# An inverse transform with cosine and sine parts held apart for half of the tokens, and mirrored tokens read backwards

## The chip, the cores and the metric

The kernel runs on one core of one Trainium2 chip. A core has a matrix engine (PE; its weight loads are listed as PEld), a vector engine (DVE), a scalar engine (ACT), a general engine (POOL) and an engine that issues transfers (SP). They run side by side, each takes its own instructions in order, and they wait for each other on semaphores. PE writes its results to PSUM, eight banks per partition, from where DVE or ACT copy or combine them; POOL and the transfers reach only SBUF. The metric is the device time of one execution in microseconds (us).

## What is computed

Attention with eight heads, and then a mixing layer that convolves along the sequence by Fourier transforms. The layer is where the change lies.

```python
def _moe_ref(x, w_proj, filter_fft, w_out):        # x: batch 4, 768 tokens, 512 channels
    proj = x @ w_proj
    x1, x2, x3 = proj[..., :D], proj[..., D:2*D], proj[..., 2*D:]
    X2 = np.fft.rfft(x2, n=S, axis=1)
    H = np.fft.rfft(filter_fft, n=S, axis=0)[None, :, :]
    x2_conv = np.fft.irfft(X2 * H, n=S, axis=1)
    y = x1 * x2_conv * x3
    return y @ w_out
```

The attention before it: scores of 768 by 768 per head, causal, and for five of the heads cut to 4 first tokens and a window of 64; exponentials, division by the row sum, product with v. All inputs are float32 in memory; the kernel computes with bfloat16 operands.

## The kernel before

**Tiling.** There are 16 head pairs (four per batch), `n` = 0 to 15, and after four of them one batch `b` of the mixing layer. For a pair, q and k are loaded, cast and transposed (T, E), scores go to PSUM in chunks (sc), ACT takes exponentials (ex), DVE masks them (mk), PE multiplies with v (at), DVE divides (rec, nm). Differences and sums of the two halves of the tokens (fd, fe and, for later pairs, fA, fS, fb, fr) go through the forward transform (W), and the same attention output is transposed for the projections (tn, te).

**The mixing layer of a batch.** The spectrum X (L1125, three pairs of tiles) is copied out (Xe) and multiplied with the filter's spectrum (pa, pb, pc), which gives P. Then, for each of four blocks `cb` of 128 channels:
- x1 and x3, projections of 768 tokens (L1160), two groups of four matmuls each;
- c, the inverse transform (L1190): two groups `r` of three matmuls, whose moving operand is the table Gi, 384 tokens wide. Group 0 gives the part of the even frequencies, group 1 that of the odd ones, each for the first 384 tokens;
- ce (a copy of group 0 from PSUM, L535 or L541) and cv (L1201): the sum of both parts is the convolution at the first 384 tokens, their difference at the last 384. They go to `conv`, for which the program lends the opening's buffer, so the trace names it turns (and the copy angle);
- g (L1179: x1 by x3) and y (L544: conv by that product) give gy; in block 3 y multiplies conv by x1 first and g (L1183) then by x3; the output matmuls (o, L1225, L1220) take gy of all four blocks, oe copies, st stores.

**What sets the order.** All operations are written as small functions with names (`c3.2.1` is batch 3, block 2, group 1), and one long table, FAST, gives the sequence in which they are issued. A letter behind a name sets the engine where there is a choice (v DVE, s ACT, p POOL, d transfer), a number behind @ which of four PSUM buffers of two banks is used from there on. Each engine gets its instructions in the order of the table. No scheduler changes it.

**The opening.** Until the first X, the tables of cosines and sines are made: DVE computes angles, wrapped angles (wrap, L676) and their size (L681), ACT takes sines (L689) and then, with another function table loaded, exponentials. The inverse table Gi comes from PE transposes of the forward one (Gt, L729) and copies (Ge). SP loads q, k and v; POOL issues the load of the filter (lfilt, L739) and of the projection weights (lw, L747). Seven blank matmuls (L580) stand at three places among the first operations. A small check of the head kinds (chk, L629 to L637, and gd at the end) decides if a general version has to run afterwards.

## Time and profile before

| | |
|---|---|
| time, median of 3 runs | 185.87 us (185.37 to 186.39) |
| profiled execution, its span | 186.0 us |
| busy: PE, DVE, ACT, POOL | 171.6, 152.5, 142.2, 83.5 us |
| inverse matmuls (L1190) | 96, PE busy 18.7 us, mean 326 ns |
| cv (L1201) | 32, DVE busy 16.4 us, mean 547 ns |
| y on POOL (L544, f_gy from turns) | 7, 11.6 us, mean 1669 ns |
| mean granted PE clock | 0.993 |

A row of the groups gives line, engine, operation, what is written and read, shapes, count, then busy time in us and the mean of one in ns, and after a second bar the engine's idle time just before and what ended it. The mean of a matmul has its way through the array in it, during which the next one runs; how long one holds PE up is read from the chain of waits, where a row gives a start, the time that passes until the next and a count. Rows of a timeline have start, length and instruction.

### The profile page before, as it was taken

The numbers are of one execution on the slowest core, as the hardware profiler recorded it, in microseconds if no ns is written. First come the engines' busy times: TensorE is split into PE (matmuls) and PEld (weight loads), VectorE is DVE, ScalarE is ACT, GpSimd is POOL, SyncE is SP. The second block draws the span as 40 slices with busy tenths as digits, with TensorE's granted clock in tenths as the row PEclk, the third lists the DMA queues.
The fourth block names the chain that finished last, engine by engine and source line by source line (L and its number), as shares of the span: only waits on it lengthen the run. The fifth ranks groups of instructions, "written<-read, shape, count | busy, mean of one in ns | idle before, by whom it ended". The sixth has DMA issues, their size and how long they took to land.

```text
span 186.0 us, 4370 instructions
## 1 busy us (share of the span) xinstructions
PE 171.6 (92%) x1685; PEld 102.2 (55%) x1702; DVE 152.5 (82%) x297; ACT 142.2 (76%) x186; POOL 83.5 (45%) x99
## 2 busy tenths in 40 slices
...
GB/s 163 305 305 194 257 272 244 260 215 130 211 224 217 104 217 222 177 149 221 216 239 201 223 203 171 127 252 222 124 102 40 118 0 131 40 4 113 188 281 108
DMA packets 76836, 33.44 MB, mean 180 GB/s; under 512 B 66058, under 2 KB 73226, under 8 KB 76810
## 3 DMA queue, kind: packets, MB, share of 16 engines
...
q8 instruction: 14, 0.23, 0.6%
q10 hardware_dynamic: 146, 0.13, 0.2%
...
HBM read 24.64 MB, written 6.29 MB: 166 GB/s over the span
## 4 chain that ended last, share of the span: by engine, by line
PE 65%; DMA 16%; ACT 4%; DVE 4%; SPq 3%; POOL 3%; issue 2%; POOLq 0%
PE f_x_ps L1160 20%; PE f_out_ps L1225 10%; PE f_X_ps L1125 10%; DMA f_filt<-in_moe_filter_fft_dram 7%; PE f_c_ps L1190 7%; PE f_sc L961 6%; PE f_att L1021 4%; DMA f_qkT<-f_qk_bf 4%; DMA f_v_f<-in_v_dram 3%; SPq L898 3%; DMA qk_ahead<-in_q_dram 2%; PE f_xt_ps L1094 2%; PE f_F_ps L768 1%; POOL f_fo L544 1%; PE f_W_ps L1082 1%
## 5 line engine op out<-in xcount | busy, mean ns | idle before, releaser
L978 ACT ACTIVATE f_pT<-f_sc 128x1024 bf16<-128x1024 f32 (+2 forms) x68 | 58.3, 914 | 4.1 <-PE f_sc L972 2.1
L1160 PE MATMUL f_x_ps<-f_xT,f_wproj 128*128 128x384 bf16 x256 | 48.4, 326 | 0.1
L1160 PEld LDWEIGHTS <-f_wproj 128*128 128x128 bf16 x256 | 23.5, 98 | 15.6 <-issue 0.4
L961 PE MATMUL f_sc<-f_qkT 64*128 64x128 bf16 (+3 forms) x328 | 21.1, 242 | 2.2 <-ACT f_pT L978 0.8
L1125 PE MATMUL f_X_ps<-f_wproj,f_xh 128*128 128x512 bf16 x91 | 22.1, 379 | 0.3
L1225 PE MATMUL f_out_ps<-f_wout,f_gy 128*128 128x512 bf16 x85 | 22.0, 379 | 0.3
L544 POOL TENSOR_TENSOR f_gy<-turns,f_gy 128x768 bf16<-128x768 bf16 x7 | 11.6, 1669 | 20.8 <-DVE f_gy L1179 11.3
L1190 PE MATMUL f_c_ps<-f_Gi,f_P 128*128 128x384 bf16 x96 | 18.7, 326 | 0.1
L1021 PEld LDWEIGHTS <-f_pT 128*128 128x128 bf16 x472 | 16.4, 97 | 4.0 <-issue 1.5
L541 ACT COPY f_o<-f_out_ps 128x1024 f32<-128x1024 f32 (+2 forms) x15 | 11.5, 788 | 8.8 <-PE f_out_ps L1225 8.8
L961 PEld LDWEIGHTS <-f_qkT 64*128 64x128 bf16 x328 | 11.1, 94 | 12.6 <-issue 8.4
L1201 DVE TENSOR_TENSOR turns<-angle,f_c_ps 128x384 bf16<-128x384 f32 x32 | 16.4, 547 | 1.7 <-ACT angle L541 1.3
L1021 PE MATMUL f_att<-f_v_aug,f_pT 128*128 128x65 bf16 x392 | 17.3, 193 | 0.4 <-DVE f_attn L1038 0.4
L544 POOL TENSOR_TENSOR f_fo<-f_attn 128x384 bf16<-128x384 bf16 x11 | 10.9, 1003 | 14.6 <-PE f_W_ps L1082 12.2
L1038 DVE TENSOR_TENSOR f_attn<-f_att,f_recs 128x768 bf16<-128x768 f32 x16 | 15.3, 954 | 0.4
L541 ACT CAST f_X<-f_X_ps 128x1024 bf16<-128x1024 f32 x11 | 11.1, 1016 | 5.9 <-PE f_X_ps L1125 5.9
L544 POOL TENSOR_TENSOR f_br<-f_fo,f_uv 128x256 bf16<-128x256 bf16 x9 | 6.9, 766 | 18.7 <-DVE f_uv L544 9.1
L1125 PEld LDWEIGHTS <-f_xh 128*128 128x128 bf16 x96 | 8.9, 98 | 10.5 <-issue 1.0
L537 POOL CAST f_qk_bf<-qk_ahead 128x768 bf16<-128x768 f32 (+1 forms) x10 | 11.4, 1149 | 4.4 <-DMA qk_ahead<-in_k_dram 4.3
L1225 PEld LDWEIGHTS <-f_gy 128*128 128x128 bf16 x92 | 8.5, 98 | 8.8 <-issue 0.4
L541 ACT CAST f_xh<-f_W_ps 128x768 bf16<-128x768 f32 x12 | 9.5, 801 | 4.6 <-PE f_W_ps L1078 4.6
L1190 PEld LDWEIGHTS <-f_P 128*128 128x128 bf16 x96 | 9.1, 98 | 6.0
...
## 6 DMA issues: line engine op xcount, KB each, us to landing
...
qk_ahead<-in_k_dram SPq DMA_DIRECT2D x6, 384.0 KB, 6.4
qk_ahead<-in_q_dram SPq DMA_DIRECT2D x6, 384.0 KB, 6.2
...
```

Of the source, the lines that this page charges most:

```text
L537: nc.gpsimd.tensor_copy(out=out, in_=in_)
L541: nc.scalar.copy(out=out, in_=in_)
L544: (nc.gpsimd if now["engine"] == "p" else nc.vector).tensor_tensor(out, a, b, op)
L961: nc.tensor.matmul(sc[:, bank, col:col + 128 * cnt], lhsT=keys, rhs=qkT(n)[rows, 0, 128 * i:128 * (i + cnt)], start=(col == 0 or not biase ...
L978: nc.scalar.activation(out=pT(n)[:, c, :, 0:w], in_=held[f"sc.{n}.{c}"][:, :, 0:w], func=AF.Exp, scale=SCALE)
L1021: nc.tensor.matmul(att[:, hh, 65 * i:65 * i + 65], lhsT=pT(n)[:, c, bank, col:col + 128], rhs=values, start=(z == 0), stop=(z == len(here) ...
L1038: nc.vector.tensor_mul(attn(n).rearrange("p i hh d -> p hh i d"), rows[:, :, :, 0:64], recs()[:, n][:, :, :, None].to_broadcast([128, 2, N ...
L1125: nc.tensor.matmul(ps[:, u, :], lhsT=xh(b)[:, cc, chain, 128 * part:128 * part + 128], rhs=wproj()[:, cc, DM:2 * DM], start=(cc == 0), sto ...
L1160: nc.tensor.matmul(ps[:, s, 0:HS], lhsT=wproj()[:, cc, part * DM + cb * 128:part * DM + (cb + 1) * 128], rhs=xT(b)[:, cc, s * HS:s * HS + HS],
L1190: nc.tensor.matmul(ps[:, r, 0:HS], lhsT=P(b)[:, t, u, ch], rhs=Gi()[:, tile_no], start=(m == 0), stop=(m == 2))
L1201: fn(conv[:, half * HS:half * HS + HS], held[f"evs.{b}.{cb}"], held[f"c_ps.{b}.{cb}"][:, 1, 0:HS])
L1225: nc.tensor.matmul(ps[:, i % 2, :], lhsT=gy(b)[:, cb, i * 128:(i + 1) * 128], rhs=wout()[:, cb, :], start=(cb == 0), stop=(cb == NC - 1))
```

## The change

The inverse transform of 384 tokens is split once more. For token t and the mirrored token 384 - t, the cosine terms agree and the sine terms are opposite at even frequencies, and the other way round at odd ones, so it is enough to compute 194 tokens (MW = 384/2 + 2), with cosine and sine parts apart, side by side in one bank. A matmul group then has two matmuls of 194 columns (one into each part) and one of 388 (for the last, mixed tile of frequencies, into both). Then, per block:
- ce copies 2 x 194 columns, cv gives two times two parts, now in a new buffer `parts`;
- cd (new) adds the two parts: tokens 0 to 193 of each half;
- cm (new) subtracts them, reads them backwards (inner step -1) and writes tokens 194 to 383 of the other half (outer step -1);
- y and g are as they were.

Gi becomes [128, 2, 4 x 194]; its tiles for mixed frequencies hold zeros in half of the partitions (gz, ga). Twelve transposes make it instead of 18; Gt1 goes, and Ge is three copies instead of two.

```diff
--- before.py
+++ after.py
@@ -61,66 +61,68 @@
 FAST = """
...
-y3.3/v o2.3.1 o2.2.1 gd3@3 gd4 x33.3.0@0 x33.3.1 g3.3 o3.0.0@2 o3.1.0@3 o3.1.1 oe2.3/s oe3.1/s o3.0.1 o3.5.0@1 st2.3
...
+cv3.0.0 o2.1.0@2 o2.0.0 o2.0.1 cv3.1.0 x33.1.1@1 cd3.0/p cv3.1.1 o2.1.1 x33.1.0 c3.2.1@0 g3.2 cd3.1/v cm3.0/p oe2.1/s
...
 """
...
@@ -362,7 +364,8 @@
     pre["identity"] = pool.tile([128, 128], BF16, name="identity")
     pre["mtab"] = pool.tile([128, 6, 128], BF16, name="mtab")
     pre["turns"] = pool.tile([128, 3, HS], I32, name="turns")
-    pre["angle"] = pool.tile([128, 3, HS], FP32, name="angle")
+    pre["flat"] = pool.tile([128, 3 * HS + 8], FP32, name="angle")
+    pre["angle"] = pre["flat"][:, 0:3 * HS].rearrange("p (m t) -> p m t", m=3)
 
     blank, table, fcol, tcol, par, tfrac, quarter, identity, mtab, turns, angle = (
         (lambda name=name: pre[name]) for name in (
@@ -514,7 +517,10 @@
             return fn
         return put
 
-    shared = {"x1s0": pre["angle"][:, 2].bitcast(BF16).rearrange("p (s t) -> p s t", s=2), "evs0": pre["angle"][:, 0], "evs1": pre["angle"][:, 1],
+    MW = HS // 2 + 2
+    flat = pre["flat"]
+    shared = {"x1s0": flat[:, 4 * MW:4 * MW + HS].bitcast(BF16).rearrange("p (s t) -> p s t", s=2),
+              "evs0": flat[:, 0:2 * MW], "evs1": flat[:, 2 * MW:4 * MW],
               "conv0": pre["turns"][:, 0].bitcast(BF16), "conv1": pre["turns"][:, 1].bitcast(BF16)}
 
     def buf(name, shape, dtype, tag=None):
@@ -547,7 +553,7 @@
     blank = lambda: pre["blank"]
     table = lambda: pre["table"]
     G = C("G", [128, 6, NM, 128], BF16)
-    Gi = C("Gi", [128, 6, NM, 128], BF16)
+    Gi = C("Gi", [128, 2, 4 * MW], BF16)
     Gk = C("Gk", [128, 2, 2, 128], BF16)
     Gh = C("Gh", [128, NM, 128], BF16, "m20")
     par = lambda: pre["par"]
@@ -719,20 +725,47 @@
         nc.vector.tensor_scalar(out=Gh()[:, :, 0:65:64], in0=G()[:, 5, :, 0:65:64], scalar1=0.5, scalar2=None,
                                 op0=ALU.mult)
 
-    for part, tiles in enumerate(((0, 1, 2, 3), (4, 5))):
-        @op(f"Gt{part}")
-        def _(part=part, tiles=tiles):
-            ps = banks(f"Gi_ps{part}", BF16)
-            for z, t in enumerate(tiles):
-                for m in range(NM):
-                    col = (z % 2) * HS + 128 * m
-                    nc.tensor.transpose(ps[:, z // 2, col:col + 128], G()[:, t, m], identity())
-
-        @op(f"Ge{part}")
-        def _(part=part, tiles=tiles):
-            rows = len(tiles) // 2
-            ev(Gi()[:, tiles[0]:tiles[-1] + 1].rearrange("p (u t) m f -> p u (t m f)", u=rows),
-               held[f"Gi_ps{part}"][:, 0:rows, 0:2 * HS])
+    @op("Gt0")
+    def _():
+        ps = banks("Gi_ps", BF16)
+        for t in range(6):
+            for m in range(2):
+                col = (t % 3) * 256 + 128 * m
+                nc.tensor.transpose(ps[:, t // 3, col:col + 128], G()[:, t, m], identity())
+
+    def mirrored(lo, hi, part):
+        return held["Gi_ps"][lo:hi, :, 0:768].rearrange("p u (k c) -> p u k c", k=3)[:, :, part, 0:MW]
+
+    @op("Ge0")
+    def _():
+        ev(Gi()[:, :, 0:2 * MW].rearrange("p u (k c) -> p u k c", k=2), mirrored(0, 128, slice(0, 2)))
+
+    @op("Ge1")
+    def _():
+        ev(Gi()[0:64, :, 2 * MW:3 * MW], mirrored(0, 64, 2))
+
+    @op("Ge2")
+    def _():
+        ev(Gi()[64:128, :, 3 * MW:4 * MW], mirrored(64, 128, 2))
+
+    def zeros(at):
+        (nc.gpsimd if now["engine"] == "p" else nc.vector).memset(at, 0.0)
+
+    @op("gz0")
+    def _():
+        zeros(Gi()[0:64, :, 3 * MW:4 * MW])
+
+    @op("gz1")
+    def _():
+        zeros(Gi()[64:128, :, 2 * MW:3 * MW])
+
+    @op("ga0")
+    def _():
+        ev(Gi()[64:65, 1, 2 * MW:3 * MW], mirrored(64, 65, 2)[:, 1])
+
+    @op("ga1")
+    def _():
+        zeros(Gi()[64:65, 1, 3 * MW:4 * MW])
 
     @op("lfilt")
     def _():
@@ -1112,7 +1145,7 @@
         return buf(f"gy.{b}", [128, NC, S], BF16, f"gy{b % 2}")
 
     SPECTRUM = (((0, 0), (0, 1)), ((1, 0), (1, 1)), ((0, 2), (1, 2)))
-    INVERSE = (((1, 0, 3), (1, 1, 4), (2, 1, 5)), ((0, 0, 0), (0, 1, 1), (2, 0, 2)))
+    INVERSE = (((1, 0), (1, 1), (2, 1)), ((0, 0), (0, 1), (2, 0)))
 
     for b in range(B):
         for t in range(3):
@@ -1186,19 +1219,36 @@
                 @op(f"c{b}.{cb}.{r}")
                 def _(b=b, cb=cb, r=r, ch=ch):
                     ps = banks(f"c_ps.{b}.{cb}")
-                    for m, (t, u, tile_no) in enumerate(INVERSE[r]):
-                        nc.tensor.matmul(ps[:, r, 0:HS], lhsT=P(b)[:, t, u, ch], rhs=Gi()[:, tile_no],
-                                         start=(m == 0), stop=(m == 2))
+                    for m, (t, u) in enumerate(INVERSE[r]):
+                        to, at = ((0, MW), (MW, 2 * MW), (0, 2 * MW))[m], (0, MW, 2 * MW)[m]
+                        nc.tensor.matmul(ps[:, r, to[0]:to[1]], lhsT=P(b)[:, t, u, ch],
+                                         rhs=Gi()[:, 1 - r, at:at + to[1] - to[0]], start=(m == 0), stop=(m == 2),
+                                         skip_group_check=True)
 
             @op(f"ce{b}.{cb}")
             def _(b=b, cb=cb):
-                ev(buf(f"evs.{b}.{cb}", [128, HS], FP32, f"evs{cb % 2}"), held[f"c_ps.{b}.{cb}"][:, 0, 0:HS])
+                ev(buf(f"evs.{b}.{cb}", [128, 2 * MW], FP32, f"evs{cb % 2}"), held[f"c_ps.{b}.{cb}"][:, 0, 0:2 * MW])
 
             for half, fn in ((0, nc.vector.tensor_add), (1, nc.vector.tensor_sub)):
                 @op(f"cv{b}.{cb}.{half}")
                 def _(b=b, cb=cb, half=half, fn=fn):
-                    conv = buf(f"conv.{b}.{cb}", [128, S], BF16, f"conv{cb % 2}")
-                    fn(conv[:, half * HS:half * HS + HS], held[f"evs.{b}.{cb}"], held[f"c_ps.{b}.{cb}"][:, 1, 0:HS])
+                    parts = buf(f"parts.{b}.{cb}", [128, 2, 2, MW], BF16, f"parts{cb % 2}")
+                    fn(parts[:, half].rearrange("p w t -> p (w t)"), held[f"evs.{b}.{cb}"],
+                       held[f"c_ps.{b}.{cb}"][:, 1, 0:2 * MW])
+
+            @op(f"cd{b}.{cb}")
+            def _(b=b, cb=cb):
+                parts = held[f"parts.{b}.{cb}"]
+                conv = buf(f"conv.{b}.{cb}", [128, S], BF16, f"conv{cb % 2}")
+                two(conv.rearrange("p (s t) -> p s t", s=2)[:, :, 0:MW], parts[:, :, 0], parts[:, :, 1], ALU.add)
+
+            @op(f"cm{b}.{cb}")
+            def _(b=b, cb=cb):
+                parts = held[f"parts.{b}.{cb}"]
+                conv = buf(f"conv.{b}.{cb}", [128, S], BF16, f"conv{cb % 2}")
+                back = HS - MW
+                two(conv.rearrange("p (s t) -> p s t", s=2)[:, ::-1, MW:HS], parts[:, :, 0, back:0:-1],
+                    parts[:, :, 1, back:0:-1], ALU.subtract)
 
             @op(f"y{b}.{cb}")
             def _(b=b, cb=cb):
```

The FAST table is a new sequence of all operations, with other engine letters at many places. Counted over the table (before, then now): y 9 on DVE and 7 on POOL, then 13 and 3; ce 10 on ACT and 6 on DVE, then 13 and 3; the new cd 9 on DVE and 7 on POOL, cm 4 and 12. Before the first X there now stand also tn3, T6, sc4.5 and sc5.2, and no longer the three matmuls of blank1, which are issued behind the second block's inverse groups of batch 0.

The first place is the opening on DVE. Before, the wrapped angles and size stood together:

```order
L676 SCALAR_TENSOR_TENSOR angle_87<-turns_86,angle_87 128x384 x3
L681 TENSOR_SCALAR f_size_159<-angle_87 128x1152
L535 COPY f_qkT_0_166<-f_qkT_ps_0_137 128x768 x2
L624 TENSOR_SCALAR f_btab_187<-mtab_85 128x768
L535 CAST f_qk_bf_1_149<-qk_ahead1_69 128x768
```

Now (names with want, zeros, local, differs and differ are chk):

```order
L682 SCALAR_TENSOR_TENSOR angle_87<-turns_86,angle_87 128x384 x3
L635 MEMSET want_61 1x8
L638 MEMSET want_61 1x1 x3
L639 TENSOR_SCALAR zeros_59<-flags_58 1x16
L641 TENSOR_TENSOR local_60<-zeros_59 1x8
L642 TENSOR_TENSOR differs_62<-local_60,want_61 1x8
L643 TENSOR_REDUCE differ_63<-differs_62 1x1
L687 TENSOR_SCALAR f_size_164<-angle_87 128x1152
L541 COPY f_qkT_0_166<-f_qkT_ps_0_148 128x768
```

Eight small instructions of chk, one of which reads a loaded input (flags), came to stand ahead of size, and a memset of v_x between the two copies of qkT.

The second place is the last batch's blocks 2 and 3 on DVE, from the end of their inverse matmuls to the last product. Before (angle is the copy ce, turns is conv, f_x1s is x1):

```order
L535 COPY angle_87<-f_c_ps_3_2_2778 128x384
L1201 TENSOR_TENSOR turns_86<-angle_87,f_c_ps_3_2_2778 128x384 x2
L535 COPY angle_87<-f_c_ps_3_3_2807 128x384
L1201 TENSOR_TENSOR turns_86<-angle_87,f_c_ps_3_3_2807 128x384 x2
L544 TENSOR_TENSOR turns_86<-turns_86,f_x1s_3_3_2751 128x768
L661 TENSOR_SCALAR other_64<-f_rows_right_2842,differ_63 1x1
L1183 TENSOR_TENSOR f_gy_3_2641<-turns_86,f_x3_ps_3_3_2845 128x768
```

Now:

```order
L1236 TENSOR_TENSOR f_parts_3_2_2855<-angle_87,f_c_ps_3_2_2824 128x388 x2
L1236 TENSOR_TENSOR f_parts_3_3_2864<-angle_87,f_c_ps_3_3_2841 128x388 x2
L550 TENSOR_TENSOR turns_86<-f_parts_3_2_2855 128x2x194
L550 TENSOR_TENSOR turns_86<-f_parts_3_3_2864 128x2x190
L550 TENSOR_TENSOR turns_86<-f_parts_3_3_2864 128x2x194
L550 TENSOR_TENSOR turns_86<-turns_86,f_x1s_3_3_2769 128x768
L550 TENSOR_TENSOR f_gy_3_2661<-turns_86,f_gy_3_2661 128x768
L1216 TENSOR_TENSOR f_gy_3_2661<-turns_86,f_x3_ps_3_3_2887 128x768
```

Both copies went to ACT; cd3.2, cm3.3, cd3.3 and the product y3.2 (the second f_gy from the end) came.

The third place is POOL's last work. Before (f_br belongs to the forward transform, f_P and f_m2 to the spectrum product):

```order
L544 TENSOR_TENSOR f_br_15_2600<-f_fo_15_2541,f_uv_15_2580 128x256
L544 TENSOR_TENSOR f_br_14_2606<-f_fo_14_2519,f_uv_14_2555 128x256
L544 TENSOR_TENSOR f_gy_2_2072<-turns_86,f_gy_2_2072 128x768
L544 TENSOR_TENSOR f_P_3_2695<-f_X_3_2_2660,f_HAB_712 128x1024
L544 TENSOR_TENSOR f_m2_3_1_2710<-f_X_3_1_2683,f_HAB_712 128x1024
L544 TENSOR_TENSOR f_gy_3_2641<-turns_86,f_gy_3_2641 128x768 x2
```

Now:

```order
L550 TENSOR_TENSOR f_P_3_2716<-f_X_3_1_2714,f_HAB_750 128x1024
L550 TENSOR_TENSOR turns_86<-f_parts_3_0_2796 128x2x194
L550 TENSOR_TENSOR turns_86<-f_parts_3_0_2796 128x2x190
L550 TENSOR_TENSOR turns_86<-f_parts_3_1_2810 128x2x190
L550 TENSOR_TENSOR f_gy_3_2661<-turns_86,f_gy_3_2661 128x768
L550 TENSOR_TENSOR turns_86<-f_parts_3_2_2855 128x2x190
```

One product of the spectrum is left, then cd3.0, cm3.0, cm3.1, y3.1 and cm3.2; y3.2 is gone from here.

More of the change, by code (lines that the diff above doesn't have):

```diff
@@ L119 @@
[L119 to L123 removed]
+turns1 ones2 turns2 angle1 ck0/p angle2 wrap0 wrap2 wrap1 mtab3 sin1 cq0/p chk T0.0@0 T0.1 ck1/p cq1/p size E0.0/v
```

119 lines of the change are left out of this document (60 added, 59 removed).

## The prediction
> **What bounds the kernel now.** I first asked for busy times in three stretches: up to the first forward-transform matmul, from there to the last matmul, and the rest. Columns: stretch and length, then busy time (and instructions) of PE, PEld, DVE, ACT and POOL, granted clock, DMA share, GB/s.
>
> ```profile
> 0.00:43.70 43.70, 36.31 (x418) 21.18 (x423) 34.46 (x65) 36.71 (x47) 20.98 (x45) 1.00 0.95 242
> 43.70:180.60 136.90, 135.28 (x1269) 81.04 (x1279) 118.02 (x233) 105.00 (x139) 62.53 (x55) 1.00 0.77 161
> 180.60:186.00 5.40, 0.01 (x1) 0.00 (x0) 0.00 (x0) 0.47 (x2) 0.00 (x0) 0.74 0.41 150
> ```
>
> PE is busy 135.3 of the middle 136.9 us at the full granted clock; DVE has 18.9 us to spare there, POOL 74. The opening is another regime: PE idles 7.4 us, DMA is 95% busy. Busy PE can hide a matmul that waits inside, so I took the chain of waits next (start, length, what).
>
> ```profile
> 19.98 13.21 DMA f_filt<-in_moe_filter_fft_dram
> 33.22 0.97 DVE f_fold L760
> 43.79 2.70 PE f_X_ps L1125 x12
> 61.53 0.67 PE f_xt_ps L1094 x12
> 62.20 1.30 PE f_x_ps L1160 x8
> 75.67 1.65 POOL f_gy L544
> 77.36 2.76 PE f_out_ps L1225 x12
> 146.21 1.95 PE f_c_ps L1190 x12
> 165.75 1.95 PE f_c_ps L1190 x12
> ```
>
> These rows have no drain in them, so they price a matmul: 1.95/12 = 162.5 ns for 384 columns, 0.67/12 = 56 ns for 128. The line through both is 0.416 ns per column plus 2.8 ns. So in the middle stretch PE really streams, and a column that is gone is time gone, as long as the feeders keep up.
>
> **What the change removes.** Per channel block the inverse transform issues six matmuls of 384 columns: 6 x 162.5 = 975 ns. After, four of 194 (83.5 ns each on that line) and two of 388 (164 ns): 662 ns. Saved: 0.313 us x 16 blocks = **-5.0 us**, all in the stretch where PE is full. Weight loads could spoil this; the transposes above load weights for every 128 columns and still go at 56 ns, so I take them as hidden under 83 ns. The bound if they are not is the mean of a load:
>
> ```profile
> L1190 PEld LDWEIGHTS <-f_P 128*128 128x128 bf16 x96 | 9.1, 98 | 6.0
> ```
>
> 98 instead of 83.5 ns, 64 times, is 0.9 us less saved. The six table transposes that go (6 x 56 ns) lie in the opening, under its waits: nothing.
>
> **What it adds.** Sixteen additions over 388 elements (nine on DVE, seven on POOL) and sixteen mirrored subtractions over 380 (four and twelve). Rows for the nearest operations, uncontended first:
>
> ```profile
> 56.98 0.35 DVE L544 TENSOR_TENSOR f_fo<-f_attn 128x384 bf16<-128x384 bf16 x1
> L544 DVE TENSOR_TENSOR f_gy<-turns,f_gy x5: 544/546/698, 71.1 to 169.5; 128x768 bf16<-128x768 bf16 x5
> L1201 DVE TENSOR_TENSOR turns<-angle,f_c_ps x32: 539/547/555, 67.3 to 173.5; 128x384 bf16<-128x384 f32 x32
> L544 POOL TENSOR_TENSOR f_fo<-f_attn 128x384 bf16<-128x384 bf16 x11 | 10.9, 1003 | 14.6 <-PE f_W_ps L1082 12.2 <-DVE f_attn L1038 2.2
> L544 POOL TENSOR_TENSOR f_gy<-turns,f_gy x7: 1634/1646/1834, 68.3 to 172.6; 128x768 bf16<-128x768 bf16 x7
> ```
>
> DVE: 0.35 us for 384 forward bf16 elements. No row reads backwards; the ends are 0.35 (as forward) and 0.547 (one element at a time, the L1201 row). I take 0.35: the only thing that differs is the sign of a step, the types are those of the 0.35 row. POOL: 1.0 us forward; if backwards cost double, 1.65 as for 768 elements; I take 1.0. Sum: DVE 13 x 0.35 = 4.6 us, POOL 19 x 1.0 = 19 us (31 at the upper end). The Trainium skill, "VectorE: DVE Perf Modes", section "Mode 2×_1P", says that two 16-bit values are taken per cycle at a step of plus or minus one. By that rule the mirrored form costs DVE its forward price; without it DVE would carry 4 x 0.2 = 0.8 us more, which its spare time hides; no row of this trace can tell.
>
> The sequence also deals work out anew; the engine letters of the table, counted, and the rows that price them:
>
> ```profile
> L544 DVE TENSOR_TENSOR f_P<-f_X,f_HAB 128x1024 bf16<-128x1024 bf16 x9 | 6.1, 680 | 0.0
> L535 DVE COPY f_qkT<-f_qkT_ps 128x768 bf16<-128x768 bf16 x6 | 5.5, 951 | 1.7 <-PE f_qkT_ps L923 1.7
> L775 DVE TENSOR_SCALAR f_HAB<-f_F_ps 128x512 bf16<-128x512 f32 x4 | 2.6, 683 | 1.0 <-PE f_sc L961 1.0
> L535 DVE CAST f_x1s<-f_x_ps 128x768 bf16<-128x768 f32 x2 | 1.9, 952 | 0.1
> ```
>
> On DVE: y +4 (0.55 each), spectrum products +4 (0.68), qkT copies +4 (0.95), scalings H -4 (0.68 and more), fd -6 (0.35), evictions of c -3 (0.55), of x1 -2 (0.95). That is 8.7 - 8.4, so DVE gains the 4.6 us of the additions and little else, and has about 122 us of work in a middle of 131: still not the bound. POOL gains at most 19 and the six fd, 25 of the 74 us that it has to spare. I cost both at nothing; the cover is DVE's remaining 9 us, and if it is gone, rival two follows. The new steps also wait inside queues that run in order. In batch 3, y3.0 on DVE waits for cm3.0 on POOL, and behind it stand cv3.2, cv3.3 and all that the last output tiles need; in batch 0, POOL's cm0.0 waits for DVE's cv, and behind it stands the cast of head pair 9, for which a transposing transfer and then score matmuls wait. Before, the same places waited for one operation less.
>
> **What it moves.** Work of 1.7 us goes from the middle into the opening: T6 and tn3 (18 transposes at 56 ns) and score chunks 4.5 and 5.2 (12 blocks of 128 columns at 56 ns). Against that three blank matmuls leave the opening for the middle (blank1, 512 columns each, 216 ns on the line above: 0.65 us). Middle: **-1.7 + 0.65**.
>
> The opening gets later. DVE now does the eight little head-type instructions (chk, first and last row below) ahead of size, and the cosines wait for size:
>
> ```profile
> qk_ahead<-in_k_dram SPq DMA_DIRECT2D x6, 384.0 KB, 6.4
> 6.40 0.76 DVE L681 TENSOR_SCALAR f_size<-angle 128x1152 int32<-128x1152 int32 x1
> 89.45 0.07 DVE L629 MEMSET want<- 1x8 f32 x1
> 90.23 0.15 DVE L637 TENSOR_REDUCE differ<-differs 1x1 f32<-1x8 f32 x1
> 7.20 0.61 ACT L689 ACTIVATE f_G<-f_size,quarter 128x384 bf16<-128x384 f32 x1
> 7.72 0.51 ACT L689 ACTIVATE f_G<-angle 128x384 bf16<-128x384 f32 x1
> 8.13 0.92 ACT L689 ACTIVATE f_G<-f_size,quarter 128x768 bf16<-128x768 f32 x1
> 9.07 1.28 ACT L978 ACT_TABLE_LOAD   x1
> 10.36 1.02 ACT L978 ACTIVATE f_pT<-f_sc 128x1024 bf16<-128x1024 f32 x1
> ```
>
> chk spans 90.38 - 89.45 = 0.93 us. Size then ends near 8.1, three cosine and sine passes (0.61 + 0.92 + 0.51) near 10.1, the table load near 11.4, and the first exponential starts 1.0 us later than at 10.36; everything of the attention queues behind it on ACT. Then SP loads one 384 KB piece (lk4) ahead of lv1, on which POOL waits before it issues the filter: 384 KB at the opening's 242 GB/s is 1.6 us. And PE has 1.7 - 0.65 - 6 x 0.056 = 0.7 us more to do. These run side by side, so they don't add up: ends 0 (hidden in PE's 7.4 us of idling) and 1.6 + 0.7 = 2.3. I take **+1.2**, a little over the ACT delay, since ACT is the fullest compute engine there (36.7 of 43.7).
>
> The end. After the last inverse matmul PE has o2.5, o2.4 and x3 of block 3 to do: 8 x 0.22 + 8 x 0.1625 = 3.0 us, then needs y3.2. DVE meanwhile runs from that matmul two cv (0.55 each), cd3.2, cm3.3, cd3.3 (0.35 each), y3.3 and y3.2 (0.55 each): 3.3 us. Before, the last steps were:
>
> ```profile
> 173.01 1.02 DVE L1201 TENSOR_TENSOR turns<-angle,f_c_ps 128x384 bf16<-128x384 f32 x2
> 174.07 0.58 DVE L544 TENSOR_TENSOR turns<-turns,f_x1s 128x768 bf16<-128x768 bf16 x1
> 175.46 0.95 DVE L1183 TENSOR_TENSOR f_gy<-turns,f_x_ps 128x768 bf16<-128x768 bf16 x1 [0.68 <-PE f_x_ps L1160]
> 179.34 0.58 ACT L541 COPY f_o<-f_out_ps 128x512 f32<-128x512 f32 x1 [0.23 <-PE f_out_ps L1225]
> 180.21 0.86 ACT L541 COPY f_o<-f_out_ps 128x512 f32<-128x512 f32 x2 [0.28 <-PE f_out_ps L1225]
> ```
>
> There DVE waited for PE (0.68 us), with y3.1 and y3.2 on POOL beside it; now PE waits for DVE, 0.3 us by the sum, 0 to 1 with hand-overs: **+0.5**. The last copy is of 512 columns (0.58 us) where it was of 256 (the second of the pair in 0.86, so 0.28): **+0.3** for copy and larger store.
>
> **Sum**, against the profiled 186.0: -5.0 - 1.7 + 0.65 + 1.2 + 0.5 + 0.3 + 0.3 (the last for the sharing of rival two, whose ends are 0 and 3.8) = -3.75, so **182.2 us**. Span and median of the runs (186.0 and 185.87) are alike, so it stands for the runs too.
>
> **Rivals.** *One, slower: the longer way from c to gy is exposed.* The two new steps lie between cv and y; where POOL has both they add 2.0 us (blocks 0.1, 0.3, 1.2, 2.3, 3.0). For it: the chain leaves PE for POOL's f_gy at 75.67 and comes back only at the first output matmul at 77.36, and POOL runs in order, so a cm may stand behind an fd. Against: PE had other work meanwhile (135.3 of 136.9), and the new order places scores, x3 and attention between c and o. If each of four batches exposed its 2.0 us, 8.0 less the 0.5 counted: 182.2 + 7.5 = 189.7. It decides from 0.95 us per batch (3.75/4).
>
> *Two, no gain: DVE and POOL hold each other up.* Rows:
>
> ```profile
> L544 DVE TENSOR_TENSOR f_fo<-f_attn 128x384 bf16<-128x384 bf16 x21 | 8.6, 423 | 0.0
> 63.23 0.82 DVE L544 TENSOR_TENSOR f_fo<-f_attn 128x384 bf16<-128x384 bf16 x1
> 63.77 0.81 POOL L544 TENSOR_TENSOR f_br<-f_fo,f_uv 128x256 bf16<-128x256 bf16 x1
> ```
>
> The same DVE operation took 0.35 alone and 0.82 beside a POOL one with two inputs. If each of POOL's 19 new instructions cost DVE 0.47, that is 9 us, all that DVE has left: DVE sets the pace, and the 3.75 are gone: 186.0. Against: of the 21 such DVE operations before (8.6 us in all, 21 x 0.35 = 7.3) few can have met one. The Trainium skill, "SBUF — State Buffer", section "Who interferes with whom", names this pair (a DVE instruction with two SBUF inputs and a GpSimd one that reads SBUF) as contending; by that rule, the trace agrees.
>
> *Three, better:* the opening hides its extra work (0), no sharing, 0.3 at the end: 182.2 - 1.2 - 0.3 - 0.2 = 180.5. *Four, the change does less than it says:* loads unhidden, 0.9 less: 183.1, inside the forecast's own range.
>
> **How the numbers follow.** Forecast with rival four 0.55 (own range 180.8 to 184.2: opening 0 to 2.3, sharing to 1), three 0.13, two 0.17, one 0.15. A measurement tells 0.5% (0.93 us) from no change. Faster: 0.55 + 0.13 + a tenth of rival two = 0.70; same 0.15; slower 0.15. Range: 179.8 to 186.4, leaving out most of rival one and little below.
>
> **What would show it.** Right: the f_c_ps group near 10.6 us of unpiled time (331 ns per three-matmul group in the chain of waits, where it was 487), the first f_X_ps near 45, the stretch from it to the last matmul near 131, PE still over 98% busy there. Rival one: PE idle before f_out_ps released by POOL turns or f_gy. Rival two: DVE over 95% busy in the middle and f_parts readers well over 0.35 us. Wrong altogether: an f_X_ps start beyond 47, or a mirrored subtraction above 0.6 us on DVE or 1.7 on POOL.

## The result

The changed kernel takes 205.4 us (median of 4, 204.4 to 207.6), the kernel before 186.1 us (185.4 to 187.2) beside it: the ratio is 1.101, its 95% interval 1.095 to 1.107. The forecast was 182.2 us in a range of 179.8 to 186.4. The profiled execution of the changed kernel has a span of 206.0 us and took 207.6 us itself, so positions in it may lie 1% late.

The chain of waits of the page, by engine, first of the kernel before:

```profile
PE 65%; DMA 16%; ACT 4%; DVE 4%; SPq 3%; POOL 3%; issue 2%; POOLq 0%
```

Busy times and the same chain after the change:

```profile
PE 175.1 (85%) x1676; PEld 103.7 (50%) x1696; DVE 177.6 (86%) x307; ACT 141.9 (69%) x189; POOL 105.5 (51%) x123
...
DVE 42%; PE 28%; ACT 9%; DMA 8%; issue 5%; POOL 4%; SPq 1%; DVEq 0%; ACTq 0%; POOLq 0%
```

The largest share of the path that sets the end went from PE to DVE, and DVE is busy 25.1 us more (152.5 before), though the sum had given it 4.6. The stretches of the prediction, at this kernel's own borders (first f_X_ps at 53.4, last matmul at 199.4):

```profile
0.00:53.40 53.40, 41.28 (x440) 24.54 (x446) 41.62 (x77) 37.50 (x50) 29.75 (x51) 0.97 0.89 213
53.40:199.40 146.00, 133.81 (x1238) 79.17 (x1251) 136.02 (x231) 103.82 (x139) 75.73 (x72) 1.00 0.68 146
199.40:206.00 6.60, 0.00 (x0) 0.00 (x0) 0.00 (x0) 0.58 (x1) 0.00 (x0) 0.89 0.31 111
```

Opening 53.4 instead of 43.7 us (+9.7), middle 146.0 instead of 136.9 (+9.1), end 6.6 instead of 5.4 (+1.2): together the 20.0 us between the spans. The granted clock of PE is 1.00 in the middle of both, so it is not a clock that makes the middle longer. In the middle DVE has 18.0 us more in two fewer instructions. Which ones became longer is seen where the same work stands on both sides; the groups by shape (count, busy us, mean ns), before:

```profile
L996 DVE TENSOR_TENSOR f_pT<-f_pT,mtab 128x1024 bf16<-128x1024 bf16 x12 | 8.5, 711 | 0.1
```

and after:

```profile
L1029 DVE TENSOR_TENSOR f_pT<-f_pT,mtab 128x1024 bf16<-128x1024 bf16 x12 | 14.1, 1179 | 0.8 <-ACT f_pT L1011 0.8
L1071 DVE TENSOR_TENSOR f_attn<-f_att,f_recs 128x768 bf16<-128x768 f32 x16 | 15.2, 953 | 0.6
L550 DVE TENSOR_TENSOR f_P<-f_X,f_HAB 128x1024 bf16<-128x1024 bf16 x10 | 9.4, 946 | 0.0
```

The mask rose from 711 to 1179 ns and the spectrum product from 680 (the prediction's row) to 946; both read two tiles of SBUF. f_attn, which reads one input from PSUM, stayed at 953 (954 before). What happens to such an instruction, in the timeline of the changed kernel on POOL and on DVE:

```profile
118.27 2.12 POOL L550 TENSOR_TENSOR f_P<-f_P,f_m 128x1024 bf16<-128x1024 bf16 x1 [1.96 <-DVE f_m L550]
118.32 2.63 DVE L550 TENSOR_TENSOR f_P<-f_X,f_HAB 128x1024 bf16<-128x1024 bf16 x1
```

POOL's product starts 0.05 us ahead and ends at 120.39. DVE's ends at 120.95, 0.56 us later: it has stood still until POOL was done, 2.63 us for work that takes 0.68. I call this the lock.

I counted it over all records (met: a two-input instruction of POOL overlaps it by over 30 ns; excess: over the tenth percentile of its shape). Before, 28 DVE instructions with two SBUF inputs were met and cost 3.3 us in excess, 91 met nothing of POOL and cost 0.4. After, 58 were met and cost 23.0 us, 74 met nothing and cost 0.6. The rest met only a cast or copy of POOL, which has one input: 13 before, for 2.6 us, and 14 after, for about 4.5. DVE instructions with an input from PSUM were met 61 and 40 times and cost under 0.5 us. So the old sequence had POOL's long instructions beside DVE's PSUM readers, and the new one has them beside its SBUF readers.

The Trainium skill, "SBUF — State Buffer", section "Who interferes with whom", says that a DVE instruction with two SBUF inputs contends with a GpSimd (POOL) instruction that reads SBUF, that the port pair which both share is an exclusive lock, and, of DVE's two-port modes, that the one that issues first holds the pair for its whole instruction and the other fully blocks. By that rule, the trace agrees: of the 58, the 33 that began behind POOL's instruction cost about 19 us, and 21 of the 25 that began ahead of it cost 0.1 us in all. The other four, with 3.7 us, had begun behind a cast, a copy or a transfer issue of POOL.

### The profile page after: what moved, and what is told of

It reads as the page before. It is cut to its first block, busy times and chain, and to the rows that moved or that the text cites. A ratio compares the mean times of both kernels' runs of the same rounds, so it can differ in the third digit from the quotient of the medians.

```text
span 206.0 us, 4408 instructions
## 1 busy us (share of the span) xinstructions
PE 175.1 (85%) x1676; PEld 103.7 (50%) x1696; DVE 177.6 (86%) x307; ACT 141.9 (69%) x189; POOL 105.5 (51%) x123
## 4 chain that ended last, share of the span: by engine, by line
DVE 42%; PE 28%; ACT 9%; DMA 8%; issue 5%; POOL 4%; SPq 1%; DVEq 0%; ACTq 0%; POOLq 0%
PE f_out_ps L1275 6%; DMA f_wout<-in_moe_w_out_dram 5%; DVE f_pT L1029 5%; DVE f_P L550 5%; DVE f_parts L1236 5%; PE f_sc L994 4%; DVE f_gy L1212 4%; DVE turns L550 4%; DMA qk_ahead<-in_q_dram 3%; PE f_X_ps L1158 3%; PE f_x_ps L1193 3%; ACT f_pT L1011 3%; DVE f_m L550 3%; DVE f_qkT L541 3%; DVE f_attn L1071 3%
## 5 line engine op out<-in xcount | busy, mean ns | idle before, releaser
L1011 ACT ACTIVATE f_pT<-f_sc 128x1024 bf16<-128x1024 f32 (+3 forms) x68 | 59.2, 913 | 11.8 <-PE f_sc L994 6.3
L994 PE MATMUL f_sc<-f_qkT 64*128 64x128 bf16 (+3 forms) x328 | 23.9, 252 | 4.8 <-DVE f_qkT L541 1.7
L550 POOL TENSOR_TENSOR turns<-f_parts 128x380 bf16<-128x380 bf16 (+1 forms) x19 | 17.6, 940 | 17.0 <-DVE f_parts L1236 16.7
L550 POOL TENSOR_TENSOR f_uv<-f_fo 128x256 bf16<-128x256 bf16 x14 | 13.7, 987 | 20.2 <-DVE f_fo L550 14.5
L550 POOL TENSOR_TENSOR f_fo<-f_attn 128x384 bf16<-128x384 bf16 x15 | 14.9, 1003 | 15.2 <-DVE f_attn L1071 9.0
L1029 DVE TENSOR_TENSOR f_pT<-f_pT,mtab 128x1024 bf16<-128x1024 bf16 (+1 forms) x18 | 20.3, 1147 | 0.8 <-ACT f_pT L1011 0.8
L1224 PE MATMUL f_c_ps<-f_Gi,f_P 128*128 128x194 bf16 (+1 forms) x96 | 14.8, 274 | 3.4 <-DVE f_gy L1212 1.1
L1236 DVE TENSOR_TENSOR f_parts<-angle,f_c_ps 128x388 bf16<-128x388 f32 x32 | 16.4, 550 | 1.2 <-PE f_c_ps L1224 0.6
L543 POOL CAST f_qk_bf<-qk_ahead 128x768 bf16<-128x768 f32 (+1 forms) x12 | 12.7, 1066 | 3.9 <-DMA qk_ahead<-in_q_dram 1.9
L541 DVE COPY f_qkT<-f_qkT_ps 128x768 bf16<-128x768 bf16 x10 | 9.2, 946 | 5.2 <-PE f_qkT_ps L956 4.1
L1275 PEld LDWEIGHTS <-f_gy 128*128 128x128 bf16 x92 | 8.3, 98 | 10.2 <-DMA f_wout<-in_moe_w_out_dram 1.3
```

Source lines behind the costliest of these rows:

```text
L541: nc.vector.tensor_copy(out=out, in_=in_)
L550: (nc.gpsimd if now["engine"] == "p" else nc.vector).tensor_tensor(out, a, b, op)
L994: nc.tensor.matmul(sc[:, bank, col:col + 128 * cnt], lhsT=keys, rhs=qkT(n)[rows, 0, 128 * i:128 * (i + cnt)], start=(col == 0 or not biase ...
L1011: nc.scalar.activation(out=pT(n)[:, c, :, 0:w], in_=held[f"sc.{n}.{c}"][:, :, 0:w], func=AF.Exp, scale=SCALE)
L1029: nc.vector.tensor_mul(some, some, tab.to_broadcast([128, 2, cols, 128]))
L1236: fn(parts[:, half].rearrange("p w t -> p (w t)"), held[f"evs.{b}.{cb}"], held[f"c_ps.{b}.{cb}"][:, 1, 0:2 * MW])
```

## The experiments

Theory L: the lock makes the loss. Rivals: the new order and its engines as such (S, O), the longer chain or the steps' own time (T, F). P stands for POOL's reading of the parts in e3, and from e13 on for PE alone as the pace; B, from e13 on, for PE and DVE in balance. Each time below is a median, and each ratio (with its 95% interval) is to runs of the kernel before on the same chip (186.0 to 187.0 us). Of the table FAST the diffs show only the operations around an edit.

**Which half of the change.** e1: the new sequence with the old transform. Where blocks 0.3, 2.2 and 2.3 now combine before the product of their buffer's earlier block has read it, they overwrite it.

```diff
-Ge0/v sc2.3@1 ck4/v ex0.4 lv3 ga0/s at0.0@2 at0.1 lq4 sc1.2@3 Ge2/s Ge1/v rec0
+Ge0/v Gt1@0 sc2.3@1 ck4/v ex0.4 lv3 at0.0@2 at0.1 lq4 sc1.2@3 Ge1/s rec0
...
-cv3.0.0 o2.1.0@2 o2.0.0 o2.0.1 cv3.1.0 x33.1.1@1 cd3.0/p cv3.1.1 o2.1.1 x33.1.0 c3.2.1@0 g3.2 cd3.1/v cm3.0/p oe2.1/s
+cv3.0.0 o2.1.0@2 o2.0.0 o2.0.1 cv3.1.0 x33.1.1@1 cv3.1.1 o2.1.1 x33.1.0 c3.2.1@0 g3.2 oe2.1/s
```

> The new sequence with the old inverse transform: the six 384-column matmuls, the second table transpose group and its copy come back, the 16 added sums (cd), 16 mirrored differences (cm) and the zeroing of the table go; everything else stands as in the changed kernel. Theory S (the new order and the new dealing-out of the engines cost the 19 us: first f_X_ps at 53.4 instead of 43.7 us, the load of f_wout issued at 78.0 instead of 63.0 us, DVE held up by POOL): 205.4 + 5.0 for the matmuls, less up to 5 for the DVE time of cd and cm: 198 to 208, first f_X_ps still beyond 50 us. Theory T (the longer way from c to gy costs it): near the kernel before, 186 to 191.

e2 and e3: the old sequence with the new transform, the steps on DVE or on the engines of the change.

```diff
-cv0.1.0 cv0.1.1 vs6/s
+cv0.1.0 cv0.1.1 cd0.1/v cm0.1/v vs6/s
```

> The old sequence and engine letters with the new inverse transform; cd and cm stand right behind the second cv of their block, all 32 on DVE. Theory S: 186.0 less 5.0 for the matmul columns, plus 0.7 at the end (two steps of 0.35 us ahead of the last product): 180 to 184; DVE carries 32 x 0.35 = 11.2 us more where it had 18.9 us to spare. Theory T: slower than before, 190 or more.

> As the run before, but cd and cm have the engines that the changed kernel gives them (cd 9 DVE and 7 POOL, cm 4 DVE and 12 POOL). Theory S: 181 to 186, the steps on POOL take 1.0 us in a chain where DVE's take 0.35. Theory P (POOL's 19 readings of parts hold DVE up and cost most of the 19 us wherever they stand): 193 or more, with DVE's instructions of two SBUF inputs well over their time before. Theory T: 190 or more.

e4: the new order with the old engine of every shared operation.

```diff
-y3.3/v oe2.5/s x33.3.1@2 y3.2/v
+y3.3/v oe2.5/s x33.3.1@2 y3.2/p
```

> The changed kernel in its own order, but every operation that both kernels have goes back to the engine that it had before (y, the copies ce, fd, fe, fA, fS, fb, spectrum products, casts, evictions); cd and cm stay as they are. If the dealing-out of engines makes the loss (DVE and POOL holding each other up): 188 to 193. If the order does (the opening's 9.7 us and the late f_wout): 198 to 208.

Measured: e1 205.2 (1.096, 1.083 to 1.109), e2 202.2 (1.081, 1.072 to 1.089), e3 209.4 (1.119, 1.107 to 1.131), e4 221.2 us (1.182, 1.171 to 1.192). Either half alone costs nearly as much as both. Neither theory fits both: S wanted 180 to 184 of e2, where the old sequence loses 15 us with the new transform in it, and T wanted 186 to 191 of e1. P's 193 or more holds in e3, but e2, where POOL reads no parts, already loses 15 us; moving the 19 steps to POOL adds 7.2. In e4 the engines can't be told from the order: the old ones are worse still in the new order, and both expected ranges lie below. The count of meetings gives a first reason: 36 in e2 with 10.2 us of excess, 44 in e3 with 16.8.

**The lock taken away.** POOL's two-input operations read a few elements (four to ten) and then write for about as long; what they compute is left out. POOL's casts and copies read as before.

```diff
     def two(out, a, b, op):
-        (nc.gpsimd if now["engine"] == "p" else nc.vector).tensor_tensor(out, a, b, op)
+        if now["engine"] == "p":
+            n = out.shape[-1]
+            few = (slice(None),) * (len(out.shape) - 1) + (slice(0, n, n // 4),)
+            nc.gpsimd.tensor_tensor(out[few], a[few], b[few], op)
+            nc.gpsimd.memset(out, 0.5)
+            nc.gpsimd.memset(out, 0.5)
+        else:
+            nc.vector.tensor_tensor(out, a, b, op)
```

> The changed kernel, but every two-input operation of POOL (61 of them, 63.7 us) reads only four or eight elements of its inputs, so that it still waits for the same writers, and then fills its output with two memsets, which take about as long but read nothing; its results are left out. Theory L (lock): a DVE instruction with two SBUF inputs that meets a reading POOL instruction stands still until that one has ended; in the changed kernel 58 of DVE's 146 such instructions met one and took 23.0 us more than their kind does alone, the 74 that met none 0.6 us more. Then DVE's busy time falls from 177.6 to 150 to 158 us and the time from 205.4 to 185 to 193. Theory O (the order: late opening, late f_wout, longer chains): DVE's long instructions are waits that move elsewhere, and the time stays at 200 or more.

> The kernel before with the same replacement of POOL's 43 two-input operations. Its 28 meetings cost DVE 3.3 us, and PE sets its pace: theory L expects 183 to 186, DVE busy 146 to 149 us. It is the base for the run with the changed kernel: theory L wants the difference of the two pairs (19 us as they are) to shrink to under 8.

> The old order with the new transform, cd and cm on DVE (202.2 us), with the same replacement. There 36 meetings cost DVE 10.2 us, the 32 new steps themselves 32 x 0.35 = 11.2 us. Theory L: the lock makes most of the 15 us over the kernel before, since it strikes in the same places as the steps: 184 to 191. Theory F (the steps' own 11.2 us, DVE being full in the stretches where they fall): 194 or more.

Measured: e5 196.2 (1.050, 1.045 to 1.055), DVE busy 157.7; e6 186.1 (0.996, 0.993 to 0.999), DVE 150.0; e7 194.3 (1.040, 1.037 to 1.044). The same groups in e5 (line numbers shifted by 7):

```profile
L1036 DVE TENSOR_TENSOR f_pT<-f_pT,mtab 128x1024 bf16<-128x1024 bf16 x12 | 8.9, 745 | 0.8 <-ACT f_pT L1018 0.8
...
L557 DVE TENSOR_TENSOR f_P<-f_X,f_HAB 128x1024 bf16<-128x1024 bf16 x10 | 6.8, 684 | 2.3 <-ACT f_X L547 2.3
```

1179 ns fell to 745, 946 to 684, and DVE lost 20 us of busy time, with POOL no less busy (112 us against 105). So most of what the long DVE instructions took is the lock's. In time, POOL's two-input reading makes 9.2 us of the changed kernel (205.4 - 196.2), and next to nothing before. But e5 stays 10 us over e6, where L wanted under 8, and e7 8.2 over it. Theory L is half of the answer: e5 lies between the ranges of L and O, and e7 in that of F. The casts still hold DVE up in these runs: instructions that met only a cast cost 4.6 us in e5 and 2.0 in e6. What that makes in time was not tested; "without the lock" below means without POOL's two-input reading.

**What the shorter matmuls are worth.** e8 and e9: the old order, the new matmuls, evictions and table; cd does four elements, cm nothing.

```diff
-                two(conv.rearrange("p (s t) -> p s t", s=2)[:, :, 0:MW], parts[:, :, 0], parts[:, :, 1], ALU.add)
+                few = slice(0, MW, 97)
+                two(conv.rearrange("p (s t) -> p s t", s=2)[:, :, few], parts[:, :, 0, few], parts[:, :, 1, few], ALU.add)
...
-                two(conv.rearrange("p (s t) -> p s t", s=2)[:, ::-1, MW:HS], parts[:, :, 0, back:0:-1],
-                    parts[:, :, 1, back:0:-1], ALU.subtract)
```

> The old order with the new matmuls, evictions and table, but cd is reduced to four elements and cm is left out (y then multiplies what is left in the buffer). It prices the matmuls alone. Theories L and F: 180 to 183 (186.0 less 5.0 for 96 shorter matmuls, plus 16 short instructions). If the shorter matmuls gain nothing in this order because something else sets the pace at once: 185 to 187.

> The old order with the new matmuls and without the new steps (195.9 us), with POOL's two-input operations turned into writes as before. In the run with reading POOL, DVE lost 8.4 us in 37 meetings, two of them over 1.8 us each just before PE's longest wait (3.6 us). Theory L: the shorter matmuls gain nothing there only because everything behind them starts earlier and meets POOL's long instructions otherwise; without the lock the 5.0 us come out: 178 to 183. If the new table and the hand-overs cost it: 187 or more.

Measured: e8 195.9 (1.052, 1.047 to 1.057), e9 188.9 (1.011, 1.004 to 1.018). Even without the steps, e8 is 5% slower than the kernel before, outside both expected ranges, and it has 37 meetings with 8.4 us. The timeline of e8 shows how a gain turns into a loss:

```profile
68.84 1.46 POOL L542 CAST f_qk_bf<-qk_ahead 128x1536 bf16<-128x1536 f32 x1
69.00 1.33 DVE L549 TENSOR_TENSOR turns<-f_parts 128x4 bf16<-128x4 bf16 x1
...
124.49 2.23 POOL L549 TENSOR_TENSOR f_P<-f_X,f_HAB 128x1024 bf16<-128x1024 bf16 x1 [1.61 <-ACT f_X L546]
124.64 2.48 DVE L549 TENSOR_TENSOR f_gy<-turns,f_gy 128x768 bf16<-128x768 bf16 x1
126.67 2.43 POOL L549 TENSOR_TENSOR f_m<-f_X,f_HAB 128x1024 bf16<-128x1024 bf16 x1
127.05 2.60 DVE L549 TENSOR_TENSOR f_P<-f_X,f_HAB 128x1024 bf16<-128x1024 bf16 x1
```

An instruction of four elements takes 1.33 us: a cast on POOL began 0.16 us ahead, and both end at 70.3. Then gy and P wait for one long POOL product each. In the kernel before, the same place reads:

```profile
121.19 0.68 DVE L544 TENSOR_TENSOR f_P<-f_X,f_HAB 128x1024 bf16<-128x1024 bf16 x1
121.57 2.28 POOL L544 TENSOR_TENSOR f_P<-f_X,f_HAB 128x1024 bf16<-128x1024 bf16 x1 [1.18 <-ACT f_X L541]
122.33 0.95 DVE L1183 TENSOR_TENSOR f_gy<-turns,f_x_ps 128x768 bf16<-128x768 bf16 x1 [0.46 <-PE f_x_ps L1160]
```

There DVE's product was already running when POOL's began, and what ran beside POOL's read PSUM. Under a microsecond of shift decides between nothing and 3.9 us (2.48 + 2.60 against 0.55 + 0.68).

In e9 no long product of POOL reads, and it still gains nothing. So I took the matmuls quite alone (e13, e14: the columns of the change from the old table, so that the transform is no longer right), and I priced DVE's spare time by doing the first cv of each block twice (e15, e16).

```diff
-                    for m, (t, u, tile_no) in enumerate(INVERSE[r]):
-                        nc.tensor.matmul(ps[:, r, 0:HS], lhsT=P(b)[:, t, u, ch], rhs=Gi()[:, tile_no],
-                                         start=(m == 0), stop=(m == 2))
+                    for m, (t, u, tile_no) in enumerate(INVERSE[r]):
+                        lo, hi = ((0, 194), (194, 388), (0, 388))[m]
+                        at = min(tile_no * HS, 6 * HS - 388)
+                        nc.tensor.matmul(ps[:, r, lo:hi], lhsT=P(b)[:, t, u, ch],
+                                         rhs=Gi().rearrange("p t m f -> p (t m f)")[:, at:at + hi - lo],
+                                         start=(m == 0), stop=(m == 2), skip_group_check=True)
```

```diff
-                    fn(conv[:, half * HS:half * HS + HS], held[f"evs.{b}.{cb}"], held[f"c_ps.{b}.{cb}"][:, 1, 0:HS])
+                    for _ in range(2 - half):
+                        fn(conv[:, half * HS:half * HS + HS], held[f"evs.{b}.{cb}"], held[f"c_ps.{b}.{cb}"][:, 1, 0:HS])
```

> The kernel before with one edit: each inverse group streams 194, 194 and 388 columns instead of three times 384 (the columns of the changed kernel, from the old table), and nothing else is changed: same evictions, same sequence, no new steps. What it leaves out: the inverse transform is no longer right. Theory P (PE alone sets the pace of the middle, and a column that is gone is time gone): 180 to 182. Theory B (PE and DVE are balanced there: what PE gains it waits for DVE): 184 to 188.

> The same with POOL's two-input operations turned into writes, so that no shift can bring a long POOL reading beside a DVE instruction. Against the kernel before with these writes (186.1, DVE 150.0 us busy): theory P 180 to 182; theory B 183 to 186.

> The kernel before with the first cv of every block done twice: 16 more DVE instructions of 0.547 us that read PSUM (8.75 us, no lock of their own), the result is the same. It prices DVE's spare time of 18.9 us in the middle. If that time is there to be used (theory P): 186 to 188. Theory B: DVE's spare time lies in places where it waits for others, and 5 us or more of the 8.75 come out: 191 or more.

> The same with POOL's two-input operations turned into writes. Theory P: 186 to 188. Theory B: the doubled cv cost about the same as with reading POOL, 190 or more. If it is the shift into the lock that costs (theory L): 186 to 188 here and 191 or more in the run before.

Measured: e13 185.7 (0.995, 0.991 to 0.999), e14 184.5 (0.987, 0.982 to 0.993), e15 199.0 (1.067, 1.062 to 1.072), e16 191.8 (1.025, 1.018 to 1.033). All four lie in theory B's ranges, though e16 doesn't cost about the same as e15, as B had it. The chain of e13's page:

```profile
PE 60%; DMA 12%; DVE 10%; ACT 4%; POOL 4%; SPq 4%; issue 3%; POOLq 0%; DVEq 0%; ACTq 0%
```

and of e14's:

```profile
PE 48%; DVE 18%; ACT 11%; POOL 10%; issue 5%; DMA 3%; POOLq 0%; DVEq 0%; ACTq 0%
```

PE's columns went, and DVE's share of the chain rose from 4 to 10 and 18% (in e14 ACT and POOL have 11 and 10% too): PE now waits for what the others deliver, DVE above all. The stretches say the same. In the middle PE is busy 132.2 us in e13 and 132.0 in e14, 3.1 and 3.2 less than without the edit, and the middle lasts 135.5 and 136.2 us, only 1.4 and 0.2 less. From the other side, 8.75 us more on DVE cost 5.7 us without the lock (191.8 - 186.1, or 0.65 us for each us) and 12.6 us with it. That price would explain e9 too: its DVE is busy 155.9 us, e14's 149.2 (the small cd, the zeros and copies of the new table, 3.4 us more of waits beside casts), and 6.7 x 0.65 = 4.4 us is the difference of the two times. This is a sum made afterwards, and no run tests it.

**The places.** e10 has the old opening (the sequence of the kernel before up to the second X group of batch 0 and the casts behind it, then the new one for what is left), e11 the early load of f_wout, e12 both, with POOL writing.

```diff
-x30.0.1@0 pa0.0/v fd5/v x30.0.0 pc0.0/v mk7.0 g0.0 x10.3.0@2 x10.3.1 x30.1.0@3 mk7.1 lk8 fS5/v fA5/p lq8 sc6.4@1
+x30.0.1@0 pa0.0/v fd5/v x30.0.0 pc0.0/v mk7.0 g0.0 x10.3.0@2 x10.3.1 x30.1.0@3 mk7.1 lk8 fS5/v fA5/p lwo lq8 sc6.4@1
...
-blank1@0 cm0.1/p xs0.2/s lq9 tn5@3 W5.0@0 tn4@2 c0.3.0@1 te4/v te5/s W5.1 ce0.3/s cd0.1/p sc6.3@3 c0.3.1 cqk9/p lwo T8
+blank1@0 cm0.1/p xs0.2/s lq9 tn5@3 W5.0@0 tn4@2 c0.3.0@1 te4/v te5/s W5.1 ce0.3/s cd0.1/p sc6.3@3 c0.3.1 cqk9/p T8
```

> The changed kernel with the old order and letters up to the second X group of batch 0 (the new table's copies stand where the old ones stood), from there its own order. The first f_X_ps is expected at 42 to 45 us instead of 53.4. If the opening's 9.7 us are a term of their own: 194 to 198. If DVE, which is over 98% busy from 120 to 170 us, takes up the gain: 200 or more.

> The changed kernel with one operation moved: POOL issues the load of f_wout behind fA5, near 67 us, where it was behind the mirrored difference cm0.1 and two casts at 78.0 us (landed at 88.2, PE waited). The first f_out_ps is expected at 82 to 85 us instead of 88.3. If that wait is a term of its own: 201 to 203.5. If DVE sets the pace behind it: 204 to 206.

> Both moves at once, and POOL's two-input operations turned into writes: the changed kernel without the three losses named so far (opening 9.7, of which 3 are lock; lock in the middle about 9; late f_wout up to 3). If these are the whole loss: 181 to 187, DVE busy under 160 us, PE over 90% busy in the span. If more is lost in the new order: 190 or more.

Measured: e10 202.7 (1.087, 1.078 to 1.095), e11 205.4 (1.101, 1.095 to 1.107), e12 192.3 us (1.030, 1.025 to 1.036). The stretches of e10:

```profile
0.00:43.20 43.20, 36.61 (x417) 21.33 (x417) 34.34 (x69) 36.68 (x48) 21.69 (x45) 1.00 1.00 241
43.20:193.40 150.20, 136.04 (x1281) 80.38 (x1279) 143.20 (x246) 104.45 (x140) 76.78 (x74) 1.00 0.72 148
```

The opening's 10.2 us are won back, and the middle grows by 4.2, with DVE at 143.2: work that the new opening had done comes back into it. The medians differ by 2.7 us, less than these two profiles (5.6): the changed kernel's was taken in its longest run, e10's in one of its two shortest. The late f_wout was no term at all: issued at 66.3 us instead of 78.0, it left the time as it was. In e11 the first f_X_ps starts at 52.3 us, with the same opening as the changed kernel, so about 1 us of the 9.7 is what one run differs from another. And e12 lies over 190, 6.2 us over e6, so more is lost in the new order than the three places.

**The remainder split.** e17 is e1 with POOL writing; e18 the changed kernel with all new steps on DVE (two of its edits are shown).

```diff
-cd0.1/p
+cd0.1/v
...
-cm0.0/p
+cm0.0/v
```

> The new sequence with the old inverse transform (205.2 us), with POOL's two-input operations turned into writes. It splits the 10.1 us that the changed kernel keeps over the kernel before when both have no lock (196.2 against 186.1): if the new order keeps them, 194 to 198; if the new steps keep them, 186 to 190.

> The changed kernel with all 32 new steps on DVE, so that POOL no longer reads parts (19 instructions, 17.6 us). Rival two as the prediction priced it (0.47 us of DVE per POOL step): 9 us come back, less 19 x 0.35 = 6.65 us of added DVE work: 202 to 204. Theory L, by POOL's reading time: DVE's loss falls by 17.6 of 63.7 parts of 23 us, 6.4 us, about what DVE takes on: 203 to 207. If the POOL steps are the main losers, by being late for y: 198 or less.

Measured: e17 199.2 (1.069, 1.060 to 1.078), e18 203.4 us (1.095, 1.089 to 1.101), with 41 meetings and 14.5 us of excess. e18 lies in the ranges of both rival two and theory L, so it doesn't tell them apart; its interval overlaps that of the changed kernel. e17 lies over the range of both expectations: the new order alone costs 13.1 us without the lock (199.2 - 186.1), and the new transform in it takes 3.0 back (196.2). In e17 PE waits once, 2.2 us, for the second copy of the table, which my edit had put there; by so much the 13.1 may be too large, and the 3.0 with it. The whole way is then 186.1 + 13.1 (order) - 3.0 (transform) + 9.2 (lock) = 205.4. In the profiles without the lock, most of what is left stands in the opening; e5 first, then e6:

```profile
0.00:50.40 50.40, 38.49 (x440) 23.36 (x446) 39.89 (x77) 37.47 (x50) 29.35 (x61) 0.93 0.90 220
50.40:187.60 137.20, 131.84 (x1238) 79.44 (x1251) 117.79 (x231) 103.16 (x139) 82.87 (x184) 1.00 0.74 158
...
0.00:42.20 42.20, 36.78 (x419) 21.84 (x425) 34.36 (x65) 36.94 (x47) 21.59 (x46) 1.00 1.00 244
42.20:178.60 136.40, 135.19 (x1269) 81.02 (x1279) 115.68 (x233) 104.83 (x139) 68.51 (x140) 1.00 0.78 164
```

8.2 us more in the opening, 0.8 in the middle. But the opening isn't a loss to be had back whole: e12, with the old one, starts f_X_ps at 44.0 us and is only 3.9 us quicker than e5 (196.2 - 192.3), because its middle is 141.0. What makes the 6.2 us that e12 keeps over e6 was not separated.

## Why the prediction was wrong, point by point

Forecast 182.2, measured 205.4 us. Three terms make most of the gap, and they overlap, so they don't add up: the columns (-5.0 in the sum, -0.6 to -1.6 measured), the lock (0.3 in the sum, 9.2 measured) and the opening (1.2 in the sum, 9.7 later). Under the first two lies one step, that only PE's stream sets the middle and that DVE's spare time covers the rest.

**"In the middle stretch PE really streams, and a column that is gone is time gone": the step that failed.** The price of a group was about right (331 ns; the chain of the changed kernel has two groups in 0.67 to 0.90 us, so 335 to 450 each):

```profile
124.62 0.90 PE f_c_ps L1224 x6
186.96 0.67 PE f_c_ps L1224 x6
```

But the -5.0 us came out as -0.6 (e13) or -1.6 (e14 against e6). PE was full, and DVE was just fast enough to keep it full. The prediction took the full engine for the only limit. With 3% of the time less to do, PE ran into the next limit, and the kernel gained under 1%.

**"I cost both at nothing; the cover is DVE's remaining 9 us": failed as well.** The prices themselves held; the rows of the tile parts after the change:

```profile
L550 POOL TENSOR_TENSOR turns<-f_parts x19: 822/880/1280, 73.0 to 191.4; 128x380 bf16<-128x380 bf16 x12, 128x388 bf16<-128x388 bf16 x7
L550 DVE TENSOR_TENSOR turns<-f_parts x13: 346/359/1002, 73.0 to 192.8; 128x388 bf16<-128x388 bf16 x9, 128x380 bf16<-128x380 bf16 x4
```

POOL's 19 steps took 17.6 us (19 forecast) and DVE's median is 359 ns (350 forecast). In e18 the 16 mirrored steps on DVE have a median of 350 ns, the 16 forward ones 353: reading backwards costs nothing. By the rule on steps of minus one that the prediction took from the Trainium skill, "VectorE: DVE Perf Modes", section "Mode 2×_1P", the trace agrees. But spare time added up over 137 us is not time to be had: e16 charges 0.65 us for each us of it, without the lock.

**Rival two: the right mechanism, counted over too few instructions.** It took the lock for a sharing, 0.47 us for each new POOL instruction, 19 times: 9 us of DVE. For those 19 the price was about right. With them off POOL (e18), DVE's excess falls by 8.5 us (23.0 to 14.5), DVE takes on the 19 steps, and 2.0 us come back (1.1 by the ratios). What it left out are the other 42 two-input instructions of POOL, which the new sequence dealt anew: 14.5 us of excess are left with them, where 43 cost 3.3 before. What counts is how many DVE instructions with two SBUF inputs begin behind any reading POOL instruction; most of them then wait for all that is left of it, up to 2 us. The forecast gave this rival 0.3 us of its 3.8.

**The opening: +1.2 in bounds of 0 to 2.3, and +9.7 measured.** Of the two delays named there, one came larger and one not at all: the first exponential starts 2.2 us later (12.6 instead of 10.4; 1.0 forecast), and the filter landed at 30.4, earlier than before (33.2), where 1.6 us of delay was forecast. The chain of waits of the changed kernel shows what was overlooked:

```profile
36.42 0.96 DVE f_qkT L541
37.38 2.03 DVE f_pT L1029
39.41 0.47 DVE f_xT L541
39.88 1.06 DVE f_fold L793
```

The folding of the filter, which before waited for its load (33.22), now stands on DVE behind the mask of head pair 5 and its exponential, and starts at 39.88, 9.4 us after the filter was there and 6.6 later than before. The mask itself takes 2.03 instead of 0.55 us, beside a product of POOL and two of its transfer issues. The order on DVE ahead of fold would have told the first part. By e10 the end gets only 2.7 us of these 9.7 back, so a sum that adds the opening at full price to the middle counts some work twice. The 1.2 was a choice between bounds that both lay too low.

**The moved -1.7 + 0.65** was not run alone; by e13 it should come out no better than the -5.0. **The end**, +0.5 and +0.3: the stretch behind the last matmul grew by 1.2, and PE's wait for y is 1.0 us, so these two were low by 1.4 together. **Rival one** (the longer way from c to gy) isn't shown: the steps do wait in it, but e18, in which they are quickest, is at most 2 us better.

**Its tests held in part.** The first f_X_ps beyond 47 us did prove the forecast wrong altogether. The sign of rival two did not show as it was written: DVE is 93% busy in the middle, not over 95 (99% from 120 to 170 us), and its readers of parts have a median of 0.36 us, with three of 13 at 0.9 to 1.0. The loss was in the readers that both kernels have, for which the sign did not ask. And one of the four mirrored steps on DVE took 0.91 us, over the 0.6 named, but beside a POOL instruction and not for its step.
